# A delta-rule attention and two MLPs on one core: a substitution walked by rows, and a held group of low parts

## The chip, the cores and the metric

One core of one Trainium2 chip runs the kernel. The metric is the device time of one execution in microseconds. Before the change three runs took 2218.66, 2220.17 and 2225.01 us, a median of 2220.17.

## The reference

The kernel computes a linear attention with a delta rule over 768 positions (4 batches, 8 heads, head size 48), then a two-layer MLP with a leaky ReLU, then eight ReLU experts whose outputs are mixed with gates that are normalised over rows and columns in turn.

```python
def _attn_ref(q, k, v, beta):
    k_n = k / (np.linalg.norm(k, axis=-1, keepdims=True) + 1e-06)
    state = np.zeros((B, H, D, D)); y = np.zeros_like(q)
    for t in range(S):
        kt, vt, bt = (k_n[:, :, t], v[:, :, t], beta[:, :, t, None])
        y[:, :, t] = np.einsum('bhd,bhde->bhe', q[:, :, t], state)
        v_old = np.einsum('bhde,bhd->bhe', state, kt)
        state = state + bt[..., None] * np.einsum('bhd,bhe->bhde', kt, vt - v_old)
    return y

x = attention, as rows of tokens [3072, 384]
x = np.maximum(0.01 * (x @ w_in), x @ w_in) @ w_out
P = exp(x @ w_gate - max); 8 times: rows / row sums, columns / column sums, * N/E
out = sum over e of P[:, e:e+1] * (np.maximum(x @ w1[e], 0) @ w2[e])
```

## The kernel before, in words

The sequence is cut into 6 steps (t = 0 to 5) of 128 positions. Within a step and batch the recurrence becomes a unit triangular system of 128x128 for each of the 8 heads. Its matrix `a` is the Gram matrix of the normalised keys, scaled by beta and masked (`part1` from line 708, the eviction at line 753): VectorE evicts the Gram products from PSUM, one instruction a head. From `a` three things are made. `a_d` collects the 32x32 diagonal blocks of all batches, copied by ScalarE and, at step 0, for half of the blocks by VectorE (`spread`, line 664; a `tensor_copy`, which the profile calls CAST). `nh` is `a` rounded to f16, with ones put on its diagonal by POOL (an affine select). `nl` is the rest, `a - nh` (`halves`, line 758), also POOL's, and it must be made before the diagonal of the same `nh` is written. The low parts are used late, in the refining product (`r_ps`); they are gathered in the list `late`.

`solve(t)` (line 776) inverts all diagonal blocks of a step at once, by forward substitution on VectorE: a transposition of `a_d` into `ld` (f16), then size - 1 steps of two instructions: `tm`, the products of a column of `ld` with a row or column of the running inverse `xs`, and `xs`, the subtraction. The blocks have 16 rows for steps 0 and 1 and 32 after that. A last transposition gives `xt`; it is recorded in the list `solved`.

`part2(t, b)` (line 806) places a batch's blocks from `xt` into a zeroed 128x128 tile with four copies (`spread` again, line 830), and transposes it with VectorE, so that both the inverse and its transpose are there (`x` and `u`). It then doubles the inverted block size with two products a round (`l_ps`): `nh` times `x`, copied to `p1` by ScalarE, then `p1` with `u`, copied into `u` and `x`. After that come the refined right-hand side, the outputs `y` and the state update.

The first MLP (`main_a`, one dense block for each step) starts as soon as the first two batches of step 0 have their `y`. Its weights come as 64-bit floats; 48 pieces are converted (`cva`, `cvs`) and split in two parts (`cvp`) by ScalarE, VectorE and POOL, stored in scratch memory by SP and loaded again as chunks `w`. The conversions may start after `solved[0]`.

All of this is recorded, not issued: a list scheduler (`Recorder`, line 294) takes every instruction's engine, inputs and estimated cost, places them by rank and writes each engine's queue in that order. AHEAD is a bonus in rank for the attention, SEED starts a jitter on the ranks. `cost` (line 357) returns as its last value whether a VectorE instruction is to keep out of POOL's way. `o.held` adds an explicit wait (line 554). While TensorE has nothing to do at the start, it runs dummy products (`stir`). Everything behind the last attention step is ordered by a second planner (`Plan`, line 62) from fixed costs: the last dense block of the first MLP, and from about 840 us the eight experts.

The lines that the prediction speaks of, as they stand before the change:

```python
            spread(t, blk, x[o:o + 32, :, o:o + 32], xt[o:o + 32, :, b * H:(b + 1) * H].rearrange("p j h -> p h j"))
        dve.transpose(out=u.rearrange("p a b -> p (a b)"), in_=x.rearrange("p a b -> p (a b)"))
...
        for o in late[0:B]:
            o.deps.add(solved[0])
            o.held.add(solved[0])
```

Of the kernel before, what the change touches and what calls it, by code (L numbers as in the profile page):

```python
# [16 lines left out]
ALU = mybir.AluOpType  # L17
# [3 lines left out]
B, H, S, D = 4, 8, 768, 48  # L21
# [25 lines left out]
SMALL = (0, 1)  # L47

STIR = (145, 20)
AHEAD, EARLY = 60.0, 60.0  # L50
ROUNDS, SEED = 10, 4
NEAR = 0.02
SLACK = 4.0
PAD = 0.07
# [239 lines left out]
class Recorder:  # L294
# [61 lines left out]
    @staticmethod  # L356
    def cost(eng, method, out, reads, kw):
        n = int(np.prod(out.shape[1:])) if isinstance(out, View) else 0
        src = [v for v in reads if isinstance(v, View)]
        psum = any(v.gen.psum for v in src)  # L360
        if eng == "PE":
            rhs = kw.get("rhs")
            if method == "transpose":
                return 0.109, 0.26, False
            if rhs.gen.rounded:
                us = 0.009 + 0.000434 * n
            elif rhs.size == 2:
                us = 0.003 + 0.000416 * n
            else:
                us = 2 * max(0.111, 0.00082 * n)  # L370
            return us, us + 0.15, False
        if method == "dma_start":
            w = next(v for v in [out] + src if isinstance(v, View) and not v.gen.dram)
            us = 0.06 + (w.parts[1] - w.parts[0]) * int(np.prod(w.shape[1:])) * w.size / 300e3
            return us if eng == "SP" else 0.06, us + 3.0, False
        if eng == "ACT":
            lat = (0.17 if psum else 0.2) + 0.00083 * n
            if not psum and len(out.shape) > 2 and out.parts[1] - out.parts[0] == 32:
                lat += 0.22
            return lat - 0.07, lat, False  # L380
        m = max([n] + [int(np.prod(v.shape[1:])) for v in src])
        if eng == "POOL":
            lat = {"tensor_tensor": 0.16 + 0.0021 * n, "affine_select": 0.17 + 0.0009 * n}.get(method, 0.15 + 0.0008 * n)
            return lat - 0.03, lat, True
        if method == "transpose":
            return 0.17 + 0.00098 * m, 0.2 + 0.00102 * m, False
        if method == "tensor_scalar":
            lat = 0.14 + 0.00056 * n
        elif method == "reciprocal":
            lat = 0.14 + 0.0064 * n  # L390
        elif method == "memset":
            lat = 0.11 + 0.00073 * n
        else:
            lat = 0.145 + 0.00104 * m
        two = not psum and (method == "tensor_scalar" or len([v for v in src if v.ids.size > 1]) > 1)
        return lat - 0.08, lat, two

    def rank(self):
# [160 lines left out]
def delta_moe_kernel(ctx: ExitStack, tc: tile.TileContext, k_l, v_l, q_l, beta_l, wa_in, wg, wc, out):  # L559
# [5 lines left out]
    pe, act, dve, pool, sp = (rec.engine(*x) for x in zip(("PE", "ACT", "DVE", "POOL", "SP"), engines))  # L565
# [96 lines left out]
    late, grams = [], []  # L662

    def spread(t, blk, out, src):
        if t == 0 and blk % 2:
            dve.tensor_copy(out=out, in_=src)
        else:
            act.activation(out=out, in_=src, func=ACTF.Copy)
# [102 lines left out]
            yield  # L771

    xt_of = {}
    marks, solved = [], []

    def solve(t):
        size = 16 if t in SMALL else 32
        nd = 32 // size

        def blocks(x):  # L780
            return x[:, 0:nd * size * 33].rearrange("p (d r) -> p d r", d=nd)[:, :, 0:size * 32].rearrange(
                "p d (c i) -> p d c i", c=size)[:, :, :, 0:size]

        ld = a1_p.tile([128, 1056], F16, tag="ld", name="ld")
        dve.transpose(out=ld[:, 0:1024], in_=a_d.rearrange("p a b -> p (a b)"))
        xs = a1_p.tile([128, 1056], F32, tag="xs", name="xs")
        pool.memset(xs, 0.0)
        pool.memset(xs[:, 0:1024:33], 1.0)
        ldb, xsb = blocks(ld).rearrange("p d i c -> p d c i"), blocks(xs)
        yield  # L790
        for j in range(size - 1):
            m = size - 1 - j
            tm = a1_p.tile([128, 1024], F32, tag="tm", name="tm")
            tv = tm[:, 0:nd * (j + 1) * m].rearrange("p (d c i) -> p d c i", d=nd, c=j + 1)
            xv = xsb[:, :, 0:j + 1, j + 1:]
            dve.tensor_tensor(out=tv, in0=ldb[:, :, j:j + 1, j + 1:].to_broadcast([128, nd, j + 1, m]),
                              in1=xsb[:, :, 0:j + 1, j:j + 1].to_broadcast([128, nd, j + 1, m]), op=ALU.mult)
            dve.tensor_tensor(out=xv, in0=xv, in1=tv, op=ALU.subtract)
            if j % 2 == 1:
                yield  # L800
        xt = a1_p.tile([128, 1024], F32, tag="tm", name="xt").rearrange("p (a b) -> p a b", a=32)
        solved.append(dve.transpose(out=xt.rearrange("p a b -> p (a b)"), in_=xs[:, 0:1024]))
        xt_of[t] = xt
        yield

    def part2(t, b):
        r = ring[(t * B + b) % RING]
        kn, kT, nh, nl = r["kn"], r["kT"], r["nh"], r["nl"]
        v, q = vs.pop((t, b)), qs.pop((t, b))
# [12 lines left out]
        xt = xt_of[t]  # L822
        u = at_p.tile([128, H, C], F16, tag="u", name="u")
        x = at_p.tile([128, H, C], F16, tag="x", name="x")
        o = pool.memset(x, 0.0)
        if t == 0 and b < 2:
            behind(o)
        for blk in range(4):
            o = 32 * blk
            spread(t, blk, x[o:o + 32, :, o:o + 32], xt[o:o + 32, :, b * H:(b + 1) * H].rearrange("p j h -> p h j"))  # L830
        dve.transpose(out=u.rearrange("p a b -> p (a b)"), in_=x.rearrange("p a b -> p (a b)"))
        yield
        for s in (16, 32, 64) if t in SMALL else (32, 64):
            pt = p1[b % 2]
# [8 lines left out]
            for i in range(nb):  # L843
                o = 2 * s * i
# [9 lines left out]
            for i in range(nb):  # L854
                o = 2 * s * i
# [13 lines left out]
        if t > 0:  # L869
            ps = bank("ks_ps")  # L870
            for p in range(NP):
# [3 lines left out]
                              op=ALU.subtract)  # L875
# [227 lines left out]
    if True:  # L1103
# [12 lines left out]
        def attention(t, b):  # L1116
            rec.bias = AHEAD
            if not b:
                for i in range(B):
                    if (t, i) not in vs:  # L1120
                        load_v(t, i)
                value_scale(t)
            if (t, b) not in qs:
                load_q(t, b)
            run(part2(t, b))
# [5 lines left out]
        dve.tensor_tensor(out=wg_r[:, :, E:2 * E], in0=wg_f[:, :, 0:E], in1=fr(wg_r[:, :, 0:E]), op=ALU.subtract)  # L1131
        run(solve(0))
        run(part1(1))
        for o in late[0:B]:
            o.deps.add(solved[0])
            o.held.add(solved[0])
        attention(0, 0)
        attention(0, 1)
        ps = phs.tile([128, TB], F32, tag="ph")
        for i in range(2):  # L1140
            for _ in range(STIR[i] // 2):
                rec.flush()
                for _ in range(2):
                    o = pe.matmul(out=ps[:, 0:256], lhsT=stir[:, 0:128], rhs=stir, start=True, stop=True)
# [50 lines left out]
        pe, act, dve, pool, sp = engines  # L1195
# [200 lines left out]
        for i in range(NF1):  # L1396
# [6 lines left out]
            if i in tasks:  # L1403
                n, t = tasks[i]
                s, j = load_step(t)
# [11 lines left out]
        for c in range(KD):  # L1417
# [5 lines left out]
            o = [None] * KD  # L1423
# [5 lines left out]
            out=cmax[:, 2 * E + t5:2 * E + t5 + 1], in_=xmax[:, t5], axis=AX.X, op=ALU.max))],  # L1429
# [277 lines left out]
        for u, (e, p) in enumerate(units):  # L1707
# [18 lines left out]
            x = [Pair(e, p, i) for i in range(4)]  # L1726
# [93 lines left out]
```

## Time and profile before

| | us |
|---|---|
| median of three runs | 2220.17 |
| lowest and highest | 2218.66, 2225.01 |
| the profiled execution, its own time | 2224.42 |
| its span, first to last instruction | 2222.7 |
| TensorE busy | 2108.3 (95%) |
| VectorE busy | 1697.5 (76%) |
| ScalarE busy | 1399.2 (63%) |
| POOL busy | 607.0 (27%) |

In the profile PE is TensorE, PEld its weight loads, DVE VectorE, ACT ScalarE, POOL GpSimd and SPq the queue that issues most DMAs. Instructions that the scheduler placed all have line 552, so they are told apart by their tiles; buffer numbers are left out of the names. The granted clock of TensorE is given as a share of full speed (1.00 is 2.4 GHz, 0.50 is 1.2 GHz). Busy times are summed over a stretch; what counts is which engine the others wait for there.

### The profile page before, as it was taken

The numbers are of one execution on the slowest core, as the hardware profiler recorded it, in microseconds if no ns is written. First come the engines' busy times: TensorE is split into PE (matmuls) and PEld (weight loads), VectorE is DVE, ScalarE is ACT, GpSimd is POOL, SyncE is SP. The second block draws the span as 40 slices with busy tenths as digits, with TensorE's granted clock in tenths as the row PEclk, the third lists the DMA queues.
The fourth block names the chain that finished last, engine by engine and source line by source line (L and its number), as shares of the span: only waits on it lengthen the run. The fifth ranks groups of instructions, "written<-read, shape, count | busy, mean of one in ns | idle before, by whom it ended". The sixth has DMA issues, their size and how long they took to land.

```text
span 2222.7 us, 42895 instructions
## 1 busy us (share of the span) xinstructions
PE 2108.3 (95%) x16963; PEld 1585.6 (71%) x16963; DVE 1697.5 (76%) x3313; ACT 1399.2 (63%) x2621; POOL 607.0 (27%) x672
## 2 busy tenths in 40 slices
PE   6688889999999999999999999999999999999999
PEld 4576767787777775767677777777777777777776
DVE  9776687658676467786877877877877878877877
ACT  5868757545656366777666656656656656656554
POOL 3644531103020052345215114214213313312200
PEclk8568889999999999999999999999999999999999
DMA  2456655466655663224333333333333323323321
GB/s 88 141 179 205 220 180 191 167 203 206 200 174 180 220 243 129 108 79 143 114 107 136 115 108 135 115 107 135 115 108 129 121 103 120 123 107 117 112 100 51
DMA packets 123450, 312.85 MB, mean 141 GB/s; under 512 B 14960, under 2 KB 66800, under 8 KB 117104
## 3 DMA queue, kind: packets, MB, share of 16 engines
q1 hardware_dynamic: 121088, 306.18, 40.2%
q10 hardware_dynamic: 2160, 3.93, 0.5%
q8 instruction: 133, 2.18, 0.4%
q14 instruction: 69, 0.57, 0.1%
HBM read 247.84 MB, written 62.13 MB: 139 GB/s over the span
## 4 chain that ended last, share of the span: by engine, by line
PE 75%; DVE 10%; ACT 6%; issue 2%; POOL 2%; DMA 1%; DVEq 0%; ACTq 0%; POOLq 0%; SPq 0%
PE b L1474 25%; PE b L1573 19%; PE ph L1573 10%; PE ph L1474 6%; PE bg L552 5%; PE po L552 4%; PE ph L552 4%; DVE tm L552 2%; DVE xs L552 2%; ACT x L552 2%; DVE gl L552 1%; ACT a_d L552 1%; DVE stir L552 1%; DVE a L552 1%; PE po L1350 1%
## 5 line engine op out<-in xcount | busy, mean ns | idle before, releaser
L1235 POOL TENSOR_TENSOR stg<-stg 128x128 f32<-128x128 f32 (+2 forms) x248 | 166.7, 690 | 805.6 <-ACT stg L1232 801.5
L1474 PEld LDWEIGHTS <-w1h 128*128 128x128 f16 x2112 | 204.8, 98 | 221.0 <-issue 1.7
L1474 PE MATMUL b<-xoh,w1h 128*128 128x512 f16 x864 | 327.5, 379 | 0.0
L1474 PE MATMUL b<-xoh,w1l 128*128 128x512 f16 x864 | 327.5, 379 | 0.0
L1474 PE MATMUL b<-xol,w1h 128*128 128x512 f16 x864 | 327.4, 379 | 0.0
L1238 DVE SCALAR_TENSOR_TENSOR acc<-b,pm,acc 128x192 f32<-128x192 f32 (+1 forms) x357 | 155.6, 449 | 92.4 <-PE b L1573 91.4
L1474 PEld LDWEIGHTS <-w1l 128*128 128x128 f16 x1056 | 103.3, 98 | 124.6
L1232 ACT ACTIVATE b<-b 128x512 f32<-128x512 f32 x144 | 84.2, 584 | 139.3 <-PE b L1474 138.1
L1238 DVE SCALAR_TENSOR_TENSOR acc<-ph,pm,acc 128x192 f32<-128x192 f32 (+1 forms) x231 | 98.1, 433 | 76.9 <-PE ph L1573 76.8
L1232 ACT ACTIVATE c<-b 128x512 f32<-128x512 f32 x192 | 113.8, 593 | 62.7 <-PE b L1474 61.7
L552 PE MATMUL ph<-x1h,w 128*128 128x512 f32 (+1 forms) x504 | 149.6, 412 | 3.1 <-ACT leak L552 2.0
L552 PE MATMUL po<-gh,w 128*128 128x512 f32 (+1 forms) x504 | 141.9, 407 | 10.8 <-ACT gh L552 10.6
L1238 DVE SCALAR_TENSOR_TENSOR c<-c,c 128x512 f32<-128x512 f32 x192 | 135.0, 720 | 6.0 <-ACT c L1232 3.7
L1235 DVE TENSOR_TENSOR c<-c,c 128x512 f32<-128x512 f32 x192 | 136.1, 712 | 2.5
L1238 DVE SCALAR_TENSOR_TENSOR c<-b,v 128x512 f32<-128x512 f32 x144 | 97.6, 689 | 43.7 <-PE b L1474 43.1
L1235 POOL TENSOR_TENSOR w2l<-stg,w2h 128x576 f16<-128x576 f32 (+1 forms) x96 | 108.6, 1151 | 81.4 <-ACT w2h L1232 81.4
L552 PEld LDWEIGHTS po<-gh,w 128*128 128x128 f32 x504 | 92.4, 199 | 28.8 <-ACT gh L552 12.3
L552 DVE TENSOR_TENSOR gl<-leak,gh 128x512 fp32r<-128x512 f32 (+1 forms) x84 | 61.1, 728 | 63.1 <-ACT leak L552 55.1
L552 PEld LDWEIGHTS ph<-x1h,w 128*128 128x128 f32 x504 | 94.5, 202 | 20.5 <-ACT leak L552 2.3
L1235 POOL TENSOR_TENSOR w1l<-stg,w1h 128x384 f16<-128x384 f32 (+1 forms) x64 | 85.9, 1348 | 34.0 <-ACT w1h L1232 34.0
L552 ACT ACTIVATE gh<-ph 128x512 fp32r<-128x512 f32 (+1 forms) x84 | 48.2, 573 | 73.5 <-PE ph L552 71.7
L1232 ACT ACTIVATE b<-ph 128x512 f32<-128x512 f32 x144 | 84.2, 585 | 6.6 <-PE ph L1474 2.5
(511 smaller groups left out, 6670.2 us busy)
## 6 DMA issues: line engine op xcount, KB each, us to landing
w<-wa_scratch SPq DMA_DIRECT2D x100, 768.0 KB, 4.8
acc_scratch<-acc SPq DMA_DIRECT2D x84, 384.0 KB, 2.6
acc<-acc_scratch SPq DMA_DIRECT2D x84, 384.0 KB, 3.5
stg<-wc SPq DMA_DIRECT2D x64, 384.0 KB, 8.7
xoh<-xo_scratch SPq DMA_DIRECT2D x21, 1152.0 KB, 5.1
xol<-xo_scratch SPq DMA_DIRECT2D x21, 1152.0 KB, 8.4
raw<-wa SPq DMA_DIRECT2D x48, 256.0 KB, 2.9
wa_scratch<-cvp SPq DMA_DIRECT2D x48, 256.0 KB, 3.4
```

The costliest lines, as they stand in the source:

```text
L552: o.last = fn(*args, **{k: x.real() if isinstance(x, View) else x for k, x in kw.items()})
L1232: return vec("ACT", n, lambda e: e.activation(out=out, in_=src, func=func, scale=scale), reads, writes, **kw)
L1235: return vec(eng, n, lambda e: e.tensor_tensor(out=out, in0=a, in1=b, op=fn), reads, writes, **kw)
L1238: return vec("DVE", n, lambda e: e.scalar_tensor_tensor(out=out, in0=a, scalar=scalar, in1=b, op0=f0, op1=f1), reads, writes, **kw)
L1350: ordered(pe.matmul(out=po[c], lhsT=self.w[wi][:, DM + c * 128:DM + (c + 1) * 128], rhs=getattr(self, n), start=i == 0 and m == 0, stop=i ...
L1474: ordered(pe.matmul(out=banks[b], lhsT=w[:, a], rhs=x[:, c].rearrange("p s k -> p (s k)"), start=start, stop=i == 2 and (a, c) == terms[-1 ...
L1573: ordered(pe.matmul(out=banks[b][:, 0:HD], lhsT=xx[:, o:o + 128], rhs=wt[:, t], start=first and k == 0 and j == 0, stop=k == NK - 1 and j ...
```

## The change

The substitution walks rows where it walked columns: the running inverse is updated below row j, for all columns up to j at once, so that columns are innermost. The column of `ld` is then repeated along the inner dimension, and the row of `xs` is read as it lies. What comes out is the transpose of what came out before, so `part2` fills `u` first and gets `x` by the transposition. The four low parts of step 0 wait for the transposition of batch 1 (`turned[1]`) and no longer for the end of the substitution. `cost` counts `tensor_copy` among the instructions that keep out of POOL's way. AHEAD and SEED are changed.

```diff
-AHEAD, EARLY = 60.0, 60.0
-ROUNDS, SEED = 10, 4
+AHEAD, EARLY = 50.0, 60.0
+ROUNDS, SEED = 10, 7
...
-        two = not psum and (method == "tensor_scalar" or len([v for v in src if v.ids.size > 1]) > 1)
+        two = not psum and (method in ("tensor_scalar", "tensor_copy") or len([v for v in src if v.ids.size > 1]) > 1)
...
-        ldb, xsb = blocks(ld).rearrange("p d i c -> p d c i"), blocks(xs)
+        ldb, xsb = blocks(ld), blocks(xs)
...
-            tv = tm[:, 0:nd * (j + 1) * m].rearrange("p (d c i) -> p d c i", d=nd, c=j + 1)
-            xv = xsb[:, :, 0:j + 1, j + 1:]
-            dve.tensor_tensor(out=tv, in0=ldb[:, :, j:j + 1, j + 1:].to_broadcast([128, nd, j + 1, m]),
-                              in1=xsb[:, :, 0:j + 1, j:j + 1].to_broadcast([128, nd, j + 1, m]), op=ALU.mult)
+            tv = tm[:, 0:nd * (j + 1) * m].rearrange("p (d i c) -> p d i c", d=nd, i=m)
+            xv = xsb[:, :, j + 1:, 0:j + 1]
+            dve.tensor_tensor(out=tv, in0=ldb[:, :, j + 1:, j:j + 1].to_broadcast([128, nd, m, j + 1]),
+                              in1=xsb[:, :, j:j + 1, 0:j + 1].to_broadcast([128, nd, m, j + 1]), op=ALU.mult)
             dve.tensor_tensor(out=xv, in0=xv, in1=tv, op=ALU.subtract)
...
-        o = pool.memset(x, 0.0)
+        o = pool.memset(u, 0.0)
...
-            spread(t, blk, x[o:o + 32, :, o:o + 32], xt[o:o + 32, :, b * H:(b + 1) * H].rearrange("p j h -> p h j"))
-        dve.transpose(out=u.rearrange("p a b -> p (a b)"), in_=x.rearrange("p a b -> p (a b)"))
+            spread(t, blk, u[o:o + 32, :, o:o + 32], xt[o:o + 32, :, b * H:(b + 1) * H].rearrange("p j h -> p h j"))
+        turned.append(dve.transpose(out=x.rearrange("p a b -> p (a b)"), in_=u.rearrange("p a b -> p (a b)")))
...
-        for o in late[0:B]:
-            o.deps.add(solved[0])
-            o.held.add(solved[0])
         attention(0, 0)
         attention(0, 1)
+        for o in late[0:B]:
+            o.deps.add(turned[1])
+            o.held.add(turned[1])
```

In the queues below a name carries its buffers: `nl0`, `nh0` belong to batch 0 of step 0, `nh4`, `nh5` to batches 0 and 1 of step 1, `u_1`, `x_1`, `p1_1` to the second of two buffers.

POOL's queue from the masks of `mt` to the first diagonal of `nh`, before:

```order
L552 AFFINE_SELECT mt_1_155<-mt_1_155 128x4x128
L552 AFFINE_SELECT mt_0_154<-mt_0_154 128x4x128 x2
L552 AFFINE_SELECT mt_1_155<-mt_1_155 128x4x128
L552 TENSOR_TENSOR nl1_0_107<-a32_1_148,nh1_0_106 128x1024
L552 TENSOR_TENSOR nl3_0_115<-uc_1_150,nh3_0_114 128x1024
L552 TENSOR_TENSOR nl0_0_103<-a32_0_147,nh0_0_102 128x1024
L552 AFFINE_SELECT nh0_0_102<-nh0_0_102 128x1024
L552 TENSOR_TENSOR cva_0_136<-cva_0_136,cvs_0_177 128x256
```

And of the change:

```order
L552 AFFINE_SELECT mt_0_154<-mt_0_154 128x4x128 x2
L552 AFFINE_SELECT mt_1_155<-mt_1_155 128x4x128 x2
L552 MEMSET xs_0_152 128x1056
L552 MEMSET xs_0_152 128x32
L552 TENSOR_TENSOR nl0_0_103<-a32_0_147,nh0_0_102 128x1024
L552 TENSOR_TENSOR nl1_0_107<-a32_1_148,nh1_0_106 128x1024
L552 TENSOR_TENSOR cva_0_136<-cva_0_136,cvs_0_177 128x256
L552 AFFINE_SELECT nh1_0_106<-nh1_0_106 128x1024
```

Two low parts instead of three stand ahead of the first diagonal; the next substitution's memset of `xs` comes ahead of them, and a product of a weight conversion comes between them and the diagonal.

VectorE's queue from the end of the first substitution, before:

```order
L552 STREAM_TRANSPOSE tm_0_153<-xs_0_152 128x1024
L552 CAST x_0_158<-tm_0_153 32x8x32 x2
L552 CAST x_1_159<-tm_0_153 32x8x32 x2
L552 STREAM_TRANSPOSE u_1_157<-x_1_159 128x1024
L552 SCALAR_TENSOR_TENSOR a32_1_148<-bg2_96,beta_64,upper_62 128x128
L552 SCALAR_TENSOR_TENSOR a32_1_148<-bg1_95,beta_64,upper_62 128x128 x3
L552 SCALAR_TENSOR_TENSOR a32_1_148<-bg2_96,beta_64,upper_62 128x128 x3
L552 SCALAR_TENSOR_TENSOR a32_1_148<-bg1_95,beta_64,upper_62 128x128
L552 STREAM_TRANSPOSE u_0_156<-x_0_158 128x1024
L552 TENSOR_SCALAR cvs_0_177<-cva_0_136 128x256
```

And of the change:

```order
L552 STREAM_TRANSPOSE tm_0_153<-xs_0_152 128x1024
L552 CAST u_1_157<-tm_0_153 32x8x32 x2
L552 CAST u_0_156<-tm_0_153 32x8x32 x2
L552 STREAM_TRANSPOSE x_1_159<-u_1_157 128x1024
L552 STREAM_TRANSPOSE x_0_158<-u_0_156 128x1024
L552 TENSOR_SCALAR cvs_0_177<-cva_0_136 128x256
L552 SCALAR_TENSOR_TENSOR a32_0_147<-po1_98,beta_64,upper_62 128x128
L552 SCALAR_TENSOR_TENSOR a32_0_147<-bg0_94,beta_64,upper_62 128x128 x3
L552 SCALAR_TENSOR_TENSOR a32_0_147<-po1_98,beta_64,upper_62 128x128 x2
```

The four copies fill `u`, both transpositions follow them at once, and the Gram tiles of step 1 come behind both and behind a conversion.

ScalarE's queue from the first `a_d` of step 1 to the first `p1` copy, before:

```order
L552 ACTIVATE a_d_0_135<-a32_1_148 32x32x8 x2
L552 ACTIVATE nh5_0_122<-a32_1_148 128x1024
L552 ACTIVATE a_d_0_135<-a32_1_148 32x32x8
L552 ACTIVATE cva_0_136<-cva_0_136 128x256
L552 ACTIVATE a_d_0_135<-a32_1_148 32x32x8
L552 ACTIVATE p1_0_0_132<-bg0_94 32x8x16
```

And of the change:

```order
L552 ACTIVATE a_d_0_135<-a32_0_147 32x32x8 x2
L552 ACTIVATE nh4_0_118<-a32_0_147 128x1024
L552 ACTIVATE a_d_0_135<-a32_0_147 32x32x8
L552 ACTIVATE cva_0_136<-cva_0_136 128x256
L552 ACTIVATE cvp_0_179<-cva_0_136 128x256
L552 ACTIVATE a_d_0_135<-a32_0_147 32x32x8
L552 ACTIVATE a_d_0_135<-a32_1_148 32x32x8
L552 ACTIVATE nh5_0_122<-a32_1_148 128x1024
L552 ACTIVATE cvp_1_180<-cva_0_136 128x256
L552 ACTIVATE p1_1_0_133<-po0_97 32x8x16
```

The first `p1` copy, now that of batch 1, has four more instructions ahead of it: one `a_d` and the `nh5` of the second Gram tile, and two `cvp`.

## Rows read from the trace of the kernel before

**Rows 1.** Stretches: us, busy of PE, PEld, DVE, ACT, POOL (count), PEclk, DMA share, GB/s.
```profile
43.00:112.00 69.00, 40.78 (x405) 34.57 (x404) 52.14 (x103) 55.18 (x130) 43.78 (x43) 0.62 0.36 113
112.00:295.00 183.00, 153.81 (x1240) 127.90 (x1238) 125.42 (x311) 134.58 (x322) 88.59 (x108) 0.83 0.62 201
295.00:420.00 125.00, 110.44 (x870) 90.49 (x870) 105.08 (x228) 72.33 (x135) 24.06 (x22) 0.95 0.53 175
420.00:795.00 375.00, 355.73 (x2684) 288.50 (x2683) 239.95 (x535) 215.83 (x403) 57.58 (x55) 0.98 0.59 198
840.00:2222.70 1382.70, 1373.72 (x11334) 988.91 (x11332) 1105.38 (x1962) 867.39 (x1544) 348.49 (x396) 1.00 0.32 113
95.00:112.00 17.00, 16.15 (x112) 15.60 (x110) 11.20 (x25) 12.82 (x29) 9.48 (x10) 0.50 0.31 101
120.00:135.00 15.00, 13.09 (x170) 12.30 (x169) 11.13 (x30) 11.03 (x30) 7.54 (x11) 0.96 0.61 194
```
**Rows 2.** The tile `cvp`: count, duration ns min/median/max, first and last start.
```profile
L552 SPq DMA_DIRECT2D wa_scratch<-cvp x48: 513/525/835, 60.2 to 280.7; - x48
```
**Rows 3.** The chain of waits from 350 to 420 us, shares by engine and tile.
```profile
by line: DVE tm L552 20.3%; ACT x L552 16.1%; DVE xs L552 14.6%; DVE stir L552 7.3%; DVE uc L552 5.4%; DVE u L552 5.2%; issue 4.3%; DVE gl L552 4.3%; PE ph L552 3.3%; DVE vsc L552 3.1%; ACT p L552 3.0%; DVE state L552 2.6%; ACT u L552 2.4%;
```
**Rows 4.** Timeline of DVE: start, us, instruction, count, idle before and releaser.
```profile
16.47 0.38 DVE L552 CAST a_d<-uc 32x256 f16<-32x256 f32 x1
...
18.80 0.60 DVE L552 CAST a_d<-uc 32x256 f16<-32x256 f32 x1
...
43.07 7.96 DVE L552 CAST x<-tm 32x256 f16<-32x256 f32 x4
...
52.30 2.12 DVE L552 SCALAR_TENSOR_TENSOR a<-bg,beta,upper 128x128 f32<-128x128 f32 x8
...
64.74 1.24 DVE L552 STREAM_TRANSPOSE x<-u 128x1024 f16<-128x1024 f16 x1
...
75.04 1.25 DVE L552 STREAM_TRANSPOSE x<-u 128x1024 f16<-128x1024 f16 x1
...
87.03 1.97 DVE L552 TENSOR_SCALAR cvs<-cva 128x256 f16<-128x256 f32 x1 [1.78 <-ACT cva L552]
```
**Rows 5.** Timeline of POOL.
```profile
18.31 1.99 POOL L552 MEMSET x<- 128x1024 f16 x2 [13.16 <-DVE a L552]
...
43.05 2.12 POOL L552 TENSOR_TENSOR nl<-a,nh 128x1024 f16<-128x1024 f32 x1 [11.67 <-DVE tm L552]
45.13 2.26 POOL L552 TENSOR_TENSOR nl<-uc,nh 128x1024 f16<-128x1024 f32 x1
47.35 2.26 POOL L552 TENSOR_TENSOR nl<-a,nh 128x1024 f16<-128x1024 f32 x1
49.68 1.11 POOL L552 TENSOR_SCALAR_AFFINE_SELECT nh<-nh 128x1024 f16<-128x1024 f16 x1
```
**Rows 6.** Timeline of PE.
```profile
50.85 0.61 PE L552 MATMUL bg<-x,nh 128*128 128x64 f16 x8 [6.27 <-POOL nh L552]
```
**Rows 7.** Timeline of ACT.
```profile
54.51 1.28 ACT L552 ACTIVATE a_d<-a 32x256 f16<-32x256 f32 x2 [5.83 <-DVE a L552]
...
55.80 1.06 ACT L552 ACTIVATE nh<-a 128x1024 f16<-128x1024 f32 x1
...
57.53 0.42 ACT L552 ACTIVATE cva<-cva 128x256 f32<-128x256 f32 x1
...
60.38 0.27 ACT L552 ACTIVATE p<-bg 32x128 f16<-32x128 f32 x1
...
65.62 1.92 ACT L552 ACTIVATE a_d<-a 32x256 f16<-32x256 f32 x3
...
68.01 0.76 ACT L552 ACTIVATE p<-bg 32x256 f16<-32x256 f32 x2
```
**Rows 8.** Timeline of DVE, the largest step of a substitution of 32 rows.
```profile
321.51 0.59 DVE L552 TENSOR_TENSOR tm<-ld,xs 128x256 f32<-128x256 f16 x1
322.14 0.43 DVE L552 TENSOR_TENSOR xs<-xs,tm 128x256 f32<-128x256 f32 x1
```

More of the change, by code (lines that the diff above doesn't have):

```diff
@@ L773, in delta_moe_kernel @@
     xt_of = {}
-    marks, solved = [], []
+    marks, solved, turned = [], [], []
     def solve(t):
```

## The prediction

> **What bounds the kernel now.** I read the stretches first [rows 1]. From 840 us to the end TensorE is busy for 1373.7 of 1382.7 us at granted clock 1.00. That part is built by another planner, which the change does not touch; it can only start earlier or later. From 420 to 795 TensorE is busy 95% of the time at 0.98. Ahead of that the limits differ. From 43 to 112 us it is busy 40.8 of 69.0 us and holds a clock of 0.62: a chain through all engines sets the pace. From 112 to 295 it is busy 84% at 0.83, while the weights are split for scratch: 48 pieces, the first stored at 60.2 us, the last at 280.7 [rows 2]. From 295 to 420 it is busy 88%, and in the second half of that the chain of waits runs through VectorE: `tm` and `xs`, the two instructions of a substitution step, hold 20.3% and 14.6% of it [rows 3]. So time is to be had before 420 us, and nearly all of it before 295.
>
> Next, VectorE where the first substitution ends [rows 4]. Four copies that place the solved blocks (a CAST of 32x256) take 7.96 us from 43.07. The same copy alone took 0.38 us at 16.47, and 0.60 beside a POOL memset at 18.80 [rows 4, 5]. In those 8 us POOL runs three low Gram parts (`nl`, 2.12 to 2.26 us each), released by the same substitution at 43.05, and then the diagonal of `nh` [rows 5]. The copies end one after another with POOL's instructions, about 2 us each instead of 0.4: the two engines exclude each other there. TensorE's first product of the block inverse waits for that diagonal and starts at 50.85 [rows 6]. ScalarE comes next: its queue has `a_d` copies ahead of the copies of that product, and those `a_d` wait for the Gram tiles that VectorE could start only at 52.30 [rows 4, 7]. So the first `p` copies end at 60.65 [rows 7].
>
> **The change, part by part.** *The walk of the substitution.* Instruction count, element count and the short lengths are the same; short rows only stand at the first steps instead of the last, which I cost at nothing because each length still occurs once. What goes is the f16 operand read at a step of 64 bytes. At 256 elements `tm` takes 0.59 us and `xs`, with no such operand, 0.43 [rows 8]: 0.16 us, or 0.63 ns an element. A substitution of 32 has the sum over j of (j+1)(31-j) = 5456 elements, 3.4 us; one of 16 with two blocks has 1360, 0.86 us. The low bound is 0 (each row is still reached by a 64-byte step); a loss is excluded, as no step has more of these than before. I take most of it: 3.0 and 0.6, since the first steps keep rows of one to three elements. The Trainium skill (SBUF — State Buffer, the note on cachelines under Door 1) has 16-byte lines and a penalty for each access that goes to a new one, which fits the 0.16 us here. By that rule only the row of one element still pays, and the sum below would be 0.7 us better.
>
> *The copies and the held low parts.* Now the low parts of step 0 wait for the transposition of batch 1, so POOL has only the memset of `xs` beside the copies. Bounds for four copies: 1.5 us (4 x 0.38) and 7.96 as now; I take 4 x 0.60 = 2.4, the row beside a memset, because that memset has the same release. From 42.4 (43.0 less 0.6) the copies end at 44.8, as do ScalarE's four. The new `x` is what the first product reads, and it comes out of a transposition (1.24 us [rows 4]): batch 1 at 46.05, batch 0 at 47.3.
>
> What the new wait holds up is POOL's queue. Two low parts, a conversion product and only then the diagonal of `nh1` stand there. The low parts run from 46.1 to 50.4. The conversion product needs VectorE: a TENSOR_SCALAR that meets a low part (one such took 1.97 us beside POOL [rows 4]; here it waits to 48.2 and ends at 48.5), eight Gram tiles of 2.12, and five conversion instructions of 1.3 in all: 51.9. POOL then adds 0.67 and 1.11. So the first product starts near 53.7, 2.9 us **later** than now. That alone decides nothing, since ScalarE is later still. Its `a_d` starts at 50.6 instead of 54.51, but five `a_d` of 0.64, two `nh` of 1.06 and three conversions of 0.42 [rows 7], 6.6 us, now precede the `p` copies; these are four of 0.27 with three conversions between and end near 59.55 instead of 60.65: 1.1 us gained. Behind them the new order is better. The next transposition of the leading batch ends at 63.6 instead of 65.98, with fewer conversions ahead of it. Its `p` copies end at 65.0 instead of 68.8, since two `a_d` stand ahead of them instead of four (the last three from 65.62 [rows 7]). The other batch's transposition ends near 71.6 instead of 76.29 [rows 4]; the eight Gram tiles that stood right before it are elsewhere. The later of the two batches decides when the first dense block may begin, so I take 4.5 us here, with 1.1 (only the first gain stays) and 6.4 (all that the copies lost) as bounds. On SP the order of the stores and loads around this is nearly unchanged; the first split piece goes out some 4 us earlier, for it waits on the same VectorE work, and no load is put behind the held step.
>
> *Which part of the later substitutions counts.* Steps 2 and 3 lie in 286 to 414, where VectorE is on the chain but TensorE is busy 88%: of 2 x 3.0 I count half, 3.0. Those after 420 lie under a TensorE busy 95%: nothing; if that cover were thinner they would give up to 6.8 more. The substitution of step 1 lies beside other work: nothing.
>
> *The reshuffle.* AHEAD, SEED and the changed port rule redraw the order up to 795 us. I cost it at zero. Its bound is a tenth of TensorE's idle time from 112 to 295 (29.2 us) either way: 3 us.
>
> **Sum:** 4.5 + 3.0 = 7.5 us. The profiled execution took 2224.42, so it would be 2216.9; it lies 4.25 above the median of the runs shown, 2220.17, and against that the forecast is **2212.7**. Its own range, from 1.1 us to 6.4 + 3.4 + 3, is 2207 to 2219. A difference of 0.3%, 6.7 us, is about what a measurement tells from none.
>
> **Rivals.** *The clock comes back.* From 95 to 112 TensorE is busy 16.2 of 17 us at 0.50 [rows 1]: the lower level of 1.2 GHz, after the thin stretch before. If the shorter chain leaves fewer gaps there, that work halves and 8.1 us go as well: 2220.2 - 15.6 = 2204.6. For: 120 to 135 shows 0.96 once the work is dense. Against: the first product comes later, so the idle time ahead of it grows.
>
> *The split weights bind.* If the 48 pieces keep their pace and end at 280.7 [rows 2], the head's 4.5 are lost and the last chunk of the first dense block comes when it does now: 2217.2. For: ScalarE, VectorE and POOL work on pieces without a break. Against: the first piece leaves late because of the same copies.
>
> *Slower: the low parts move onto the conversions.* Held, they run beside VectorE's conversion instructions, which exclude POOL as the copies did. Should the five of them and the TENSOR_SCALAR each wait out a POOL instruction (1.97 against 0.3), that is 10 us on VectorE, and POOL's own product and the diagonal wait for it. The first product then comes near 62, and what lies beyond decides once it comes after 57, where ScalarE would be ready. The `p` copies end some 4 us late, and if 120 to 135, now 13.1 us busy at 0.96, falls to the lower level as well, 13 more less its 1.9 idle: 4 + 11 - 3 gives 2232. For: POOL's order has that conversion product ahead of the diagonal. Against: by the times above those five start when both low parts are over. The Trainium skill (SBUF — State Buffer, Who interferes with whom) says that a VectorE instruction with two SBUF inputs and a POOL instruction that reads SBUF keep each other out; by it this case needs only that they meet.
>
> *The walk gains nothing,* if a step to a new row costs what a step to a new element did: 3.0 and the 0.6 in the 4.5 are lost, 2216.3.
>
> **How the numbers follow.** Forecast 0.50, of which two thirds lie beyond 0.3% (0.34); clock 0.19; split weights 0.14; slower 0.13; no gain of the walk 0.04. Faster: 0.34 + 0.19 = 0.53. Same: 0.16 + 0.14 + 0.04 = 0.34. Slower: 0.13. The range leaves out the slower case and the far end of the clock case: 2200 to 2226, the ends being the clock case less, and the split-weights case plus, some of the reshuffle (4.6 and 8.8 us).
>
> **What would show it.** The four copies near 0.4 to 0.6 us each; `tm` of 256 elements near 0.43; both low parts after the first transposition; the first product near 53 to 54 and the second batch's transposition near 72. Wrong: copies still near 2 us, `tm` unchanged, a first `p` copy later than 60, or the last split piece stored at 280 or later.

## The result, and the profile after

The changed kernel takes 2193.61 us, the median of four runs (2192.51 to 2196.31), beside 2220.66 for the kernel before: a ratio of 0.9877, 95% interval 0.986 to 0.9895. That is 27 us, 3.6 times the forecast and below the range. The profiled execution took 2192.51 us, its span is 2190.5. The one profiled before took 2224.42, so the two traces lie 32 us apart where the medians lie 27 apart: some 5 us of what they show is the choice of the execution and not the change.

The same stretches as [rows 1], of the changed kernel (us, busy of PE, PEld, DVE, ACT, POOL, granted clock, DMA share, GB/s):

```profile
43.00:112.00 69.00, 44.77 (x427) 38.83 (x427) 49.78 (x121) 59.15 (x142) 42.31 (x44) 0.62 0.44 136
112.00:295.00 183.00, 156.23 (x1302) 129.06 (x1302) 134.07 (x333) 143.66 (x329) 98.27 (x111) 0.86 0.62 199
295.00:420.00 125.00, 115.79 (x914) 94.84 (x913) 93.39 (x219) 74.61 (x144) 14.75 (x18) 0.97 0.64 215
420.00:795.00 375.00, 360.02 (x2678) 289.96 (x2678) 248.06 (x538) 223.46 (x411) 78.15 (x71) 1.00 0.61 205
840.00:2190.50 1350.50, 1342.25 (x11205) 972.45 (x11203) 1084.83 (x1928) 848.63 (x1510) 343.14 (x392) 1.00 0.32 112
95.00:112.00 17.00, 15.67 (x117) 14.85 (x118) 11.40 (x31) 14.01 (x42) 9.12 (x11) 0.50 0.49 153
```

The first four rows cover 752 us in both kernels. TensorE's idle time in them is 91.2 us before (28.2, 29.2, 14.6, 19.3) and 75.2 after (24.2, 26.8, 9.2, 15.0). What the lower clock level costs, busy time times one less the granted clock, is 54.2 before (15.5, 26.1, 5.5, 7.1) and 42.4 after (17.0, 21.9, 3.5, 0). Together 28 us less, of the 32 between these two executions: idle time gives 16, the clock 12 (with the clock in two digits, the second is good to some 2 us). Only 2.5 of the 28 lie before 112 us, where the forecast saw most; 7.4 lie in 295 to 420 and 11.4 after 420, where it saw little and nothing.

The start itself went as forecast. VectorE, POOL, TensorE and ScalarE, which answer to [rows 4 to 7]:

```profile
40.93 1.25 DVE L552 STREAM_TRANSPOSE tm<-xs 128x1024 f32<-128x1024 f32 x1
42.28 2.21 DVE L552 CAST u<-tm 32x256 f16<-32x256 f32 x4
44.52 2.37 DVE L552 STREAM_TRANSPOSE x<-u 128x1024 f16<-128x1024 f16 x2
...
42.30 1.22 POOL L552 MEMSET xs<- 128x1056 f32 x2 [11.42 <-DVE tm L552]
45.85 4.25 POOL L552 TENSOR_TENSOR nl<-a,nh 128x1024 f16<-128x1024 f32 x2 [2.33 <-DVE x L552]
...
53.44 0.61 PE L552 MATMUL po<-x,nh 128*128 128x64 f16 x8 [8.61 <-POOL nh L552]
...
58.47 0.55 ACT L552 ACTIVATE p<-po 32x128 f16<-32x128 f32 x2
```

The four copies take 2.21 us for 7.96 (forecast 2.4), the low parts start at 45.85 (46.1), the first product at 53.44 (53.7), the first four `p` copies end at 59.02 (59.55). The first product of the dense block, `ph<-x1h,w`, starts at 109.8 us for 115.1. The steps of the substitution, as in [rows 8]: the first and the last step of the fourth and of the fifth one, then the largest step of the third:

```profile
351.28 0.16 DVE L552 TENSOR_TENSOR tm<-ld,xs 128x31 f32<-128x31 f16 x1
...
386.19 0.19 DVE L552 TENSOR_TENSOR tm<-ld,xs 128x31 f32<-128x31 f16 x1
...
504.39 0.20 DVE L552 TENSOR_TENSOR tm<-ld,xs 128x31 f32<-128x31 f16 x1
...
545.78 0.19 DVE L552 TENSOR_TENSOR tm<-ld,xs 128x31 f32<-128x31 f16 x1
...
297.81 0.41 DVE L552 TENSOR_TENSOR tm<-ld,xs 128x256 f32<-128x256 f16 x1
298.40 0.41 DVE L552 TENSOR_TENSOR xs<-xs,tm 128x256 f32<-128x256 f32 x1
```

`tm` of 256 elements falls from 0.59 to 0.41, equal to `xs`. The first and the third row are first steps, 31 rows of one element; they take 0.16 and 0.20 us, the last steps, one row of 31, take 0.19 both times. The last split piece goes out at 266.5 for 280.7 [rows 2], and VectorE's part of the chain from 350 to 420, 20.3% and 14.6% before [rows 3], is now:

```profile
by line: PE ph L552 26.7%; PE po L552 24.6%; PE bg L552 20.4%; DVE tm L552 5.7%; DVE xs L552 5.6%; DVE stir L552 3.2%; DVE uc L552 3.0%; issue 2.2%; DVE state L552 2.0%; DVE gl L552 1.7%; DVE n L552 1.6%; DVE rn L552 1.6%; DVE vsc L552 0.9%
```

More of that fall is the new order's than the walk's: with the walk by rows in the old order (below), the two still hold 13.0% and 12.4% of this stretch.

### The profile page after: what moved, and what is told of

Read it like the earlier page. It is cut to its first block, busy times and chain, and to the rows that moved or that the text cites. A ratio compares the mean times of both kernels' runs of the same rounds, so it can differ in the third digit from the quotient of the medians.

```text
span 2190.5 us, 42910 instructions
## 1 busy us (share of the span) xinstructions
PE 2094.0 (96%) x16963; PEld 1574.8 (72%) x16963; DVE 1675.6 (76%) x3313; ACT 1400.3 (64%) x2621; POOL 606.1 (28%) x672
## 4 chain that ended last, share of the span: by engine, by line
PE 78%; DVE 10%; ACT 6%; issue 3%; POOL 2%; DMA 1%; DVEq 0%; POOLq 0%; ACTq 0%
PE b L1474 25%; PE b L1573 19%; PE ph L1573 11%; PE bg L552 6%; PE ph L1474 6%; PE po L552 5%; PE ph L552 5%; DVE tm L552 2%; ACT u L552 2%; DVE xs L552 1%; DVE a L552 1%; PE ph L1326 1%; DVE gl L552 1%; ACT p L552 1%; DVE cva L552 1%
## 5 line engine op out<-in xcount | busy, mean ns | idle before, releaser
L1232 ACT ACTIVATE c<-b 128x512 f32<-128x512 f32 x192 | 113.9, 593 | 62.9 <-PE b L1474 61.9
L552 PE MATMUL ph<-x1h,w 128*128 128x512 f32 (+1 forms) x504 | 144.7, 403 | 3.7 <-ACT leak L552 2.1
```

The source lines that it names most:

```text
L552: o.last = fn(*args, **{k: x.real() if isinstance(x, View) else x for k, x in kw.items()})
L1232: return vec("ACT", n, lambda e: e.activation(out=out, in_=src, func=func, scale=scale), reads, writes, **kw)
```

## The experiments

Ratios are to the kernel before, run beside each on the same chip (its median there lay between 2222.2 and 2225.2 us). Eighteen kernels ran, in five groups.

### The walk alone, in a fixed order

The walk changes nothing that the scheduler counts, so every queue keeps its order when it alone is exchanged: the traces of each pair have the same instructions in the same order on every engine. First in the kernel before:

```diff
-        ldb, xsb = blocks(ld).rearrange("p d i c -> p d c i"), blocks(xs)
+        ldb, xsb = blocks(ld), blocks(xs)
...
-            xv = xsb[:, :, 0:j + 1, j + 1:]
+            xv = xsb[:, :, j + 1:, 0:j + 1]
```

> The kernel before, every queue in its old order, with the substitution alone walked by rows (what is placed afterwards is then the transpose of what it should be, so this kernel's output is not the reference's; instructions, sizes and order stay). Three theories for the 27 us. Order theory (most of it is the redrawn order of the scheduler): the walk gives what the forecast took for it, 3 to 5 us, so 2216 to 2218. Walk theory (the substitutions are on the path everywhere, so all of 4 x 3.4 + 2 x 0.86 = 15.3 us comes off): near 2205. Wait theory (the held low parts give most of it, through the start): like the order theory here, 2216 to 2218, with the four copies still near 8 us. In all of them tm of 256 elements falls from 0.59 to 0.43 us.

Measured 2208.89 us, ratio 0.9943 (0.993 to 0.9956): 12.7 us faster. The reverse edit in the changed kernel:

> The changed kernel, every queue in its new order, with the substitution alone walked by columns again (here too the placed blocks are the transposes of what they should be, and the output is not the reference's). Order theory and wait theory: 3 to 5 us slower than the changed kernel, 2197 to 2199, ratio to before near 0.990. Walk theory: 15 us slower, near 2209, ratio near 0.995. tm of 256 elements back at 0.59 us.

Measured 2205.42, ratio 0.9924 (0.991 to 0.9938), 0.0047 above the changed kernel's 0.9877: 10.4 us. So the walk is worth 10 to 13 us in either order, near the walk theory's 15 and far from 3 to 5. For the kernel before, all instructions `tm` and `xs` are (columns: count | busy us, mean ns | idle before):

```profile
L552 DVE TENSOR_TENSOR tm<-ld,xs 128x31 f32<-128x31 f16 (+20 forms) x154 | 72.5, 471 | 2.3 <-ACT x L552 0.3
L552 DVE TENSOR_TENSOR xs<-xs,tm 128x31 f32<-128x31 f32 (+20 forms) x154 | 55.9, 363 | 2.2
```

and with the walk by rows in the old order:

```profile
L552 DVE TENSOR_TENSOR tm<-ld,xs 128x31 f32<-128x31 f16 (+20 forms) x154 | 57.9, 376 | 2.3 <-ACT x L552 0.4
L552 DVE TENSOR_TENSOR xs<-xs,tm 128x31 f32<-128x31 f32 (+20 forms) x154 | 55.0, 357 | 2.2
```

VectorE saves 14.6 us in `tm`, and 12.7 us reach the end. Where they come can be read from the transposition that ends a substitution (here the third to the sixth), and from the first product of the second planner's part. The kernel before:

```profile
347.33 1.20 DVE L552 STREAM_TRANSPOSE tm<-xs 128x1024 f32<-128x1024 f32 x1
...
413.60 1.25 DVE L552 STREAM_TRANSPOSE tm<-xs 128x1024 f32<-128x1024 f32 x1
...
570.69 1.25 DVE L552 STREAM_TRANSPOSE tm<-xs 128x1024 f32<-128x1024 f32 x1
...
685.96 1.25 DVE L552 STREAM_TRANSPOSE tm<-xs 128x1024 f32<-128x1024 f32 x1
...
767.04 0.50 PE L1326 MATMUL ph<-x1h,w 128*128 128x512 f32 x1
```

With the walk by rows, same order:

```profile
340.53 1.20 DVE L552 STREAM_TRANSPOSE tm<-xs 128x1024 f32<-128x1024 f32 x1
...
403.82 1.25 DVE L552 STREAM_TRANSPOSE tm<-xs 128x1024 f32<-128x1024 f32 x1
...
556.54 1.25 DVE L552 STREAM_TRANSPOSE tm<-xs 128x1024 f32<-128x1024 f32 x1
...
669.47 1.25 DVE L552 STREAM_TRANSPOSE tm<-xs 128x1024 f32<-128x1024 f32 x1
...
751.50 0.50 PE L1326 MATMUL ph<-x1h,w 128*128 128x512 f32 x1
```

The lead is 6.8, 9.8, 14.2 and 16.5 us at the four transpositions, and 15.5 where the second planner begins. It grows on after 420 us, under a TensorE that is busy 95%. But it is read from one execution each, and such a lead holds the difference between two executions too: the kernel of the next section, which has the old walk and the old order and a median only 1.5 us off, has a lead of 8.5 us at the third transposition in its profiled execution, its fastest of eleven. So the 6.8 us, of which VectorE had saved 4.4 by then, can't be put down to the walk; how the lead grows behind it is the better sign. The same transpositions in the new order, the fourth to the sixth, with the walk by columns:

```profile
390.79 1.24 DVE L552 STREAM_TRANSPOSE tm<-xs 128x1024 f32<-128x1024 f32 x1
...
554.75 1.25 DVE L552 STREAM_TRANSPOSE tm<-xs 128x1024 f32<-128x1024 f32 x1
...
674.09 1.25 DVE L552 STREAM_TRANSPOSE tm<-xs 128x1024 f32<-128x1024 f32 x1
```

and in the changed kernel:

```profile
387.13 1.24 DVE L552 STREAM_TRANSPOSE tm<-xs 128x1024 f32<-128x1024 f32 x1
...
546.71 1.25 DVE L552 STREAM_TRANSPOSE tm<-xs 128x1024 f32<-128x1024 f32 x1
...
662.60 1.25 DVE L552 STREAM_TRANSPOSE tm<-xs 128x1024 f32<-128x1024 f32 x1
```

Here the lead is 3.7, 8.0 and 11.5 us, and 0.5 at the third. From the fourth transposition to the sixth it grows by 6.7 us in the old order and by 7.8 in the new one, where VectorE saves 7.0 and 6.5 in the two substitutions between.

### The wait alone, in a fixed order

In the changed kernel the explicit wait is left out and the order kept; in the kernel before it is added and the order kept (the instructions are issued in another interleaving, which leaves each engine's queue as it was). The first of the two edits:

```diff
         for o in late[0:B]:
             o.deps.add(turned[1])
-            o.held.add(turned[1])
```

> The changed kernel in its own order, with the wait of the four low parts on the second transposition left out (nothing they read depends on it); they start when POOL's queue comes to them, near 43.5 us, right behind the memset. Order theory and walk theory: two of the four copies and perhaps the two transpositions each wait out a low part of 2.1 us, so VectorE is 4 to 6 us later with the Gram tiles of step 1, but POOL is done with the low parts earlier; 0 to 4 us slower, 2194 to 2198. Wait theory: at least 10 us slower, 2204 or more.

Measured 2192.86, ratio 0.9871 (0.9857 to 0.9885): no difference from the changed kernel that the two intervals, some 5 us together, could tell. The copies are held again, and both transpositions end 3.9 us later:

```profile
42.31 6.09 DVE L552 CAST u<-tm 32x256 f16<-32x256 f32 x4
48.43 2.37 DVE L552 STREAM_TRANSPOSE x<-u 128x1024 f16<-128x1024 f16 x2
...
43.45 4.34 POOL L552 TENSOR_TENSOR nl<-a,nh 128x1024 f16<-128x1024 f32 x2
```

Its first product of the dense block comes at 112.7 us, 2.9 later than with the wait, and its end comes no later.

> The kernel before in its own order and with the old walk, with one wait added: the low parts of step 0 wait for the transposition of batch 1 (only they; no queue is reordered). In all theories the four copies fall from 7.96 to about 2.4 us and the transposition ends near 46.8; but three low parts of 2.2 us now stand between it and the diagonal of nh0, so the first product starts near 55.7 instead of 50.85. Order theory and walk theory: what the copies give is lost to the later diagonal, 0 to 4 us slower or no change, 2219 to 2225. Wait theory: 10 us or more faster, 2211 or less.

Measured 2220.73, ratio 0.9997 (0.9987 to 1.0007): 0.7 us faster, between 2.9 faster and 1.6 slower. VectorE, POOL and TensorE:

```profile
43.23 1.55 DVE L552 CAST x<-tm 32x256 f16<-32x256 f32 x4
...
50.62 1.24 DVE L552 STREAM_TRANSPOSE u<-x 128x1024 f16<-128x1024 f16 x1
51.78 1.04 DVE L552 TENSOR_SCALAR cvs<-cva 128x256 f16<-128x256 f32 x1
...
50.55 2.13 POOL L552 TENSOR_TENSOR nl<-a,nh 128x1024 f16<-128x1024 f32 x1
...
54.03 0.61 PE L552 MATMUL bg<-x,nh 128*128 128x64 f16 x8 [9.31 <-POOL nh L552]
```

The copies shrink from 7.96 to 1.55 us, the first product moves from 50.85 to 54.03, the first product of the dense block from 115.1 to 112.9, and the time stays within its interval. The wait theory, 10 us or more, falls with both runs: the stalled copies were real and worth little at the end. That the 2.2 us of the dense block come out there is not excluded by the interval; a gain as large as the forecast's 4.5 is.

### The numbers, with and without the new edges

The "edges" are the new dependence of the low parts and the exchange of `u` and `x`; the "numbers" are AHEAD, SEED and the port rule in `cost`.

```diff
-AHEAD, EARLY = 50.0, 60.0
-ROUNDS, SEED = 10, 7
+AHEAD, EARLY = 60.0, 60.0
+ROUNDS, SEED = 10, 4
...
-        two = not psum and (method in ("tensor_scalar", "tensor_copy") or len([v for v in src if v.ids.size > 1]) > 1)
+        two = not psum and (method == "tensor_scalar" or len([v for v in src if v.ids.size > 1]) > 1)
```

> The walk by rows and the held low parts of the change, with AHEAD 60, SEED 4 and the old port rule. The first four runs put the walk at 10.5 to 12.6 us in a fixed order and the wait at nothing, so some 15 us are in the order. Numbers theory (AHEAD, SEED and the rule made that order): this stays near the walk's gain, 2206 to 2211, ratio 0.993 to 0.996. Edges theory (the new dependence of the low parts and the exchange of u and x made it): near 2194, ratio 0.988.

Measured 2201.74, ratio 0.9902 (0.9886 to 0.9919), between the two: 0.0041 below the walk alone. The same numbers, put the other way round into the kernel before:

> The kernel before with AHEAD 50, SEED 7 and the new port rule alone; the walk by columns and the hold on the end of the substitution stay. Numbers theory: near 2205, ratio 0.992 to 0.993, as the changed kernel with the walk by columns. Edges theory: no change, 2216 to 2226. Scatter theory (any edit draws a new order, good or bad by some 10 us, and this one draws again): anything from 2205 to 2230.

Measured 2206.35, ratio 0.9923 (0.9908 to 0.9938), as the numbers theory had it, and equal to the changed kernel with the walk by columns (0.9924). Then two other seeds of the changed kernel (`SEED` 4 and 5 for 7):

> The changed kernel with SEED 4 in place of 7 alone. Scatter theory (the order is a lucky draw): 5 to 15 us slower, 2198 to 2209. If AHEAD 50 and the port rule make the order good under any seed: within 4 us of 2193.6, 2190 to 2198.

> The changed kernel with SEED 5. As for seed 4: scatter theory 2198 to 2209, otherwise 2190 to 2198.

Measured 2189.87, ratio 0.9846 (0.9831 to 0.9862), and 2208.9, ratio 0.9932 (0.9913 to 0.9951). The seed alone moves the time by 19 us. Seed 4 came out where an order that is good under any seed would put it, seed 5 where a lucky draw would: neither theory holds for both. Seed 4 is at least as good as the change's own 7; its interval just touches that of the changed kernel, and it is the fastest version measured.

### How far a seed moves the kernel before

Each run changes SEED alone, from 4 to 7, 5, 8 and 9; for the first:

```diff
-ROUNDS, SEED = 10, 4
+ROUNDS, SEED = 10, 7
```

> The kernel before with SEED 7 in place of 4, nothing else. So far, with the walk's 12 us taken out, the orders drawn stand at 0 (the kernel before), -10 (old numbers, new edges), -17 (new numbers with seed 7, either edges), -22 (seed 4) and -3 us (seed 5). Draw theory (the numbers mean nothing by themselves; the order of the kernel before was a poor draw): 5 to 20 us faster, 2203 to 2218, ratio 0.991 to 0.998. Numbers theory (AHEAD 50 and the port rule make the order good): 2216 to 2230, ratio 0.998 to 1.004.

> The kernel before with SEED 5. Draw theory: spread over 2200 to 2225, on the mean of the four seeds some 8 us faster than before. Numbers theory: the four seeds lie around the kernel before, 2216 to 2232, the mean within 4 us of it.

> The kernel before with SEED 8, a third order drawn with the old numbers. Draw theory: spread over 2200 to 2225. Numbers theory: 2216 to 2232.

> The kernel before with SEED 9, a fourth order drawn with the old numbers. Draw theory: spread over 2200 to 2225. Numbers theory: 2216 to 2232.

Measured, in this order: 0.9977 (0.9961 to 0.9993), 1.0066 (1.0043 to 1.009), 1.0006 (0.9991 to 1.0021), 0.9986 (0.9973 to 0.9999). The mean of these is 1.0009, so the order of the kernel before was no poor draw, and the draw theory falls in that point. The seeds themselves spread over 0.9%, 20 us.

### AHEAD and the port rule apart

AHEAD 50 alone, at four seeds:

```diff
-AHEAD, EARLY = 60.0, 60.0
+AHEAD, EARLY = 50.0, 60.0
```

> The kernel before with AHEAD 50 for 60 alone (seed 4). AHEAD theory (the smaller bonus for the attention makes the order better): 8 to 17 us faster, ratio 0.992 to 0.9965. Rule theory (the port rule made it) or draw theory: within the scatter of the four seeds, ratio 0.996 to 1.008.

> The kernel before with AHEAD 50 and SEED 7, the port rule old: the new numbers without the rule. With the rule this was at 0.9923; with AHEAD 60 at 0.9977. AHEAD theory: 0.991 to 0.994. Rule theory: 0.996 to 0.999.

> The kernel before with AHEAD 50 and SEED 5; at AHEAD 60 this seed was at 1.0066. AHEAD theory: 0.997 to 1.001. Draw theory: anywhere from 0.996 to 1.007.

> The kernel before with AHEAD 50 and SEED 8; at AHEAD 60 this seed was at 1.0006. AHEAD theory: 0.993 to 0.997. Draw theory: anywhere from 0.996 to 1.007.

Measured 0.9945 (0.993 to 0.996) at seed 4, 0.9993 (0.9982 to 1.0005) at 7, 1.0054 (1.0033 to 1.0075) at 5, 0.9992 (0.9983 to 1.0002) at 8. Against AHEAD 60 at the same seeds that is -0.55, +0.16, -0.12 and -0.14%: no effect beyond the draws. Then AHEAD 50 with the rule, at seeds 4 and 5:

> The kernel before with AHEAD 50, SEED 4 and the new port rule; walk and hold as before. Without the rule this was at 0.9945; the whole change at this seed at 0.9846, which is 0.990 when the walk's 0.005 is taken out. Rule theory: 0.988 to 0.991. Edges theory: 0.993 to 0.996. Draw theory: anywhere from 0.991 to 1.004.

> The kernel before with AHEAD 50, SEED 5 and the new port rule. Without the rule this was at 1.0054; the whole change at this seed at 0.9932, or 0.998 without the walk. Rule theory: 0.997 to 1.000. Edges theory: 1.003 to 1.007. Draw theory: anywhere from 0.991 to 1.007.

Measured 0.9895 (0.988 to 0.991) and 0.9994 (0.9985 to 1.0003), both where the rule theory had them. All at AHEAD 50:

| seed | before | with the port rule | the whole change |
|---|---|---|---|
| 4 | 0.9945 | 0.9895 | 0.9846 |
| 5 | 1.0054 | 0.9994 | 0.9932 |
| 7 | 0.9993 | 0.9923 | 0.9877 |

From the first column to the second the time falls by 0.50, 0.60 and 0.70%; from the second to the third by 0.49, 0.62 and 0.46%, which is what the walk alone gave (0.57 and 0.47%). So the edges add nothing at these seeds. At AHEAD 60 and seed 4, with the old rule, they came with 0.41% on top of the walk alone (0.9902 against 0.9943), no more than a seed moves. How the rule helps is open. It concerns the 16 copies of step 0 alone, and not by the stall that it is written against: at seed 7 with the rule the four copies are still held by POOL,

```profile
43.31 6.14 DVE L552 CAST x<-tm 32x256 f16<-32x256 f32 x4
```

against 7.96 without it, and a longer relief of these copies in a fixed order gave no gain that could be measured. What it certainly does is draw another order. Three pairs agree, but two orders from one kernel can differ by that much as well.

## Why the prediction was wrong

The direction was right, and nearly every event of the first 75 us. The sum failed in all three of its terms.

**Later substitutions: "those after 420 lie under a TensorE busy 95%: nothing", and half of steps 2 and 3.** This step failed by 7 to 9 us: 3.6 was put down with the 0.6 of the first substitution, the walk gave 10 to 13 in all. Over the last two substitutions, where the forecast had nothing, the lead grew by 6.7 and 7.8 us in the two orders. The prediction had named 6.8 for a thinner cover and then left it out of the bounds of its sum. The size of the saving was right (13.2 us forecast on VectorE as 4 x 3.0 + 2 x 0.6, 14.6 measured). Wrong was to price its place by TensorE's busy share. The chain of the kernel before had the answer, and I read it only from 350 to 420. For 316 to 420, 420 to 560 and 560 to 767 it reads (one line for each stretch, in that order):

```profile
by line: DVE tm L552 20.8%; DVE xs L552 13.8%; ACT x L552 12.0%; DVE stir L552 7.3%; DVE gl L552 6.9%; issue 6.2%; DMA x_scratch<-leak 6.1%; DVE uc L552 3.6%; DVE u L552 3.5%; PE ph L552 2.2%; DVE vsc L552 2.1%; ACT p L552 2.0%; DVE a L552 
...
by line: PE ph L552 23.7%; PE bg L552 22.9%; PE po L552 19.1%; DVE tm L552 6.7%; DVE xs L552 5.0%; DVE stir L552 2.4%; DVE gl L552 2.1%; issue 2.0%; ACT a_d L552 1.9%; DVE kn L552 1.6%; DVE a L552 1.6%; DVE x1l L552 1.3%; DVE xmax L552 1.3%
...
by line: PE bg L552 19.1%; PE po L552 18.7%; PE ph L552 14.5%; DVE tm L552 8.8%; DVE xs L552 6.4%; ACT x L552 5.8%; ACT a_d L552 5.1%; DVE gl L552 3.1%; DVE stir L552 2.8%; issue 2.4%; ACT gh L552 1.9%; ACT nh L552 1.5%; ACT leak L552 1.5%;
```

`tm` holds 20.8% of 104 us, 6.7% of 140 and 8.8% of 207: 21.6 + 9.4 + 18.2 = 49.2 us of the path. It became shorter by 14.6 of 72.5, a fifth: 9.9 us, near what was measured. The working was made after the result, so the other order is the better test. The chain from 0 to 800 us in one piece, for the kernel before and for the changed kernel with the walk by columns:

```profile
by line: PE bg L552 14.9%; PE po L552 11.7%; PE ph L552 11.4%; DVE tm L552 6.6%; DVE xs L552 4.6%; ACT x L552 4.3%; issue 4.2%; DVE gl L552 2.8%; ACT a_d L552 2.1%; DVE stir L552 2.1%; DVE a L552 2.0%; DVE cva L552 1.6%; DMA x_scratch<-leak
...
by line: PE bg L552 13.6%; PE po L552 13.3%; PE ph L552 11.4%; issue 6.8%; DVE tm L552 6.7%; DVE xs L552 4.8%; ACT u L552 4.1%; DVE a L552 3.1%; DMA x_scratch<-leak 2.3%; DVE gl L552 2.2%; ACT p L552 1.9%; ACT cva L552 1.8%; DVE cva L552 1.
```

`tm` holds 52.8 and 53.6 us; a fifth of either is 10.6 to 10.7, against 12.7 and 10.4 measured. A TensorE that is busy 95% still stood idle for 19.3 us after 420. With the walk by rows in the old order the rows from 295 to 420 and from 420 to 795 are:

```profile
295.00:420.00 125.00, 114.91 (x930) 92.73 (x928) 101.04 (x232) 80.82 (x151) 24.45 (x24) 1.00 0.57 190
420.00:795.00 375.00, 360.48 (x2692) 292.46 (x2691) 239.71 (x544) 218.65 (x405) 66.63 (x60) 0.98 0.61 206
```

After 420 the idle time fell to 14.5 us and the clock stayed at 0.98; from 295 to 420 the idle time fell from 14.6 to 10.1 and the clock rose from 0.95 to 1.00. Whether the walk brought that rise is not shown, for in the new order the clock of this stretch is 0.97 with either walk.

**The reshuffle: "I cost it at zero. Its bound is ... 3 us."** This failed most, by 17 us: AHEAD, SEED and the port rule alone, in the kernel before, gave 0.9923. The bound was a tenth of an idle time, taken from one trace of one order, and no row supports it. Nine orders with the old walk and the old rule (five seeds at AHEAD 60, four at 50) lie between 0.9945 and 1.0066: 27 us from best to worst. Why one order is better than another is not shown. In the runs' terms the change is -0.07% for AHEAD 50 with seed 7, -0.70 for the rule and -0.46 for the walk with the edges: -1.23%, 27 us. These are differences of ratios at one seed, each good to some 0.2%.

**The copies and the held low parts: 4.5 us.** The events were right to about 1 us, up to the other batch's last transposition at 70.59 (71.6 forecast). Their worth was not: the dense block started 5.3 us earlier, but the walk and the new numbers, each put in alone, make up the 27 us without the edges (and the numbers alone start it at 107.6 us). A relief that brings it forward by 2 to 3 us showed no gain at the end in either order, to within 2 us in the old one and 5 in the new. Nor does its start tell the total elsewhere: the changed kernel starts it at 113.9 us with seed 4 (2189.87 us) and at 105.4 with seed 5 (2208.9). Where the lead is lost is seen in part. From 200 to 300 us the kernel without the wait was granted 0.97, with it 0.90, so a lead of 2.9 us was made up; why the clock differs there is not shown, and it is one execution each.

**The rivals.** The clock did not come back where I looked, at 95 to 112 (0.50 in both), but further on, and the split weights did not bind: their last store moved by 14.2 us. The low parts did not run into the conversions. As "would show it" I had named four signs of the start and one of the walk. All came out, and none of them could tell a gain of 7 us from one of 27.

The rule for rows of one element in the Trainium skill (SBUF — State Buffer, the note on cachelines under Door 1) would have a first step dearer than the last one of the same size. The traces leave that open: the first steps took 0.16 and 0.20 us where the last took 0.19, and 0.20 and 0.21 where the last took 0.19 in the kernel before with the walk by rows. At the prediction's 0.63 ns an element, 31 elements make 0.02 us, which is no more than these rows differ among themselves.

## What to carry to other kernels

Price a shorter instruction by its part of the chain of waits over all of the time in which it runs, not by how busy the engine beside it is: here that came within 3 us in two orders, and 5% idle of 375 us was enough to let the last two substitutions pay nearly in full. Where a scheduler writes the order, an edit's own worth is measured with the order kept, and what a new order can be worth is judged by the scatter of a few orders, here 27 us from best to worst, before any sum is made; the rule's orders went beyond that, so it is no bound. A stall that vanishes at the start of a long kernel is a gain only if a run in a fixed order shows the end moving. And a lead read from two traces is that of two executions; the medians decide.

## What the runs showed of the hardware

Of VectorE's instructions beside the same POOL instruction some are held and some are not. With the low part from 50.55 to 52.68, the transposition at 50.62 took 1.24 us, as it does alone, while the TENSOR_SCALAR behind it took 1.04 us and ended 0.14 us behind POOL, against 0.25 in the kernel before, where no low part ran beside it. The copies too are held: four took 6.09 us beside the low parts, 1.55 without POOL. That agrees with the Trainium skill (SBUF — State Buffer, Who interferes with whom), which counts casts and `tensor_scalar` among the instructions that can take the ports shared with POOL; I had cited it for two inputs only, and a copy has one.
